# A gated spectral filter and MLP: exchange of partition halves by transfers within SBUF, one unsplit tile, outputs weighed early

## The chip, the cores and the metric

The kernel runs on one core of one Trainium2 chip. A core has five engines with an instruction queue each: PE (TensorE, matrix products into the banks of PSUM), DVE (VectorE), ACT (ScalarE), POOL (GpSimd) and SP (SyncE). SP, ACT and POOL also issue DMA transfers, which 16 DMA engines carry out. The metric is the device time of one execution in microseconds. A shape such as 128x512 is partitions by elements of a partition.

## The reference

The input is one sequence of 2048 tokens of width 512; F is 1792.

```
x = A_x
g = sigmoid((x * gate_w).sum(-1, keepdims=True))
a = irfft2(rfft2(x) * (w_r + 1j * w_i))             # over both axes
b = gelu(x @ w1 + b1) @ w2 + b2                     # tanh form of gelu
return g * a + (1 - g) * b
```

So one branch is a two-dimensional Fourier transform, a product with a filter and the transform back; the other is an MLP; a gate for each token mixes them. All values are fp32.

## The kernel before

**Numbers.** An fp32 operand is split into a high part that the fast product format fp32r holds and a low part, the difference. A product is then three fast matmuls: high by high, high by low, low by high. The high part is made by a copy (`split`, `copy`, L424), the low part by a subtraction (L466). Some products of the transform take plain fp32 operands instead.

**Order.** The kernel writes out all of its work as steps (`add`, `v` for DVE, `a` for ACT, `m` for PE, `dma` and `store` for SP, `acc` for an adding transfer on POOL), each with the tiles that it reads and writes. The string ORDER holds the order in which the numbered steps are emitted, and SLOTS the buffer of each tile. The costs and lags in the calls were for the search that made ORDER; when the kernel runs, each engine takes its own steps strictly in the order given and waits at each for what it reads. The order of one engine against another is set by semaphores alone.

**Tiling.** The 2048 tokens are 16 blocks j of 128. They stand in four chunks c = j mod 4 of 512 tokens: CA is chunks 0 and 1, CB is 2 and 3. F is 14 tiles f of 128, the model width is four quarters q of 128.

**The Fourier branch.** `forward(j)` loads a block (L477, the first two in halves, L502 and L504), adds and subtracts its quarters on DVE (`eo` L575, `w` L578), multiplies by a table `cf` on PE (`pd`, plain fp32), splits that into `zb` (L608, L612) and multiplies by a table for the block (`py`) into Y[j]. The columns of the gate's weights are written into `cf` by a small DVE copy (L529), so that `pd` gives the gate's sums as well; that copy waits for both halves of `cf` (L509). `stage1`, `filt` and `stage4` combine blocks four at a time on DVE. `own_rows` sends partitions 0 and 64 of all Y, which hold special rows, through a small matmul of their own (L636, L652).

`inverse(c, h)` takes two blocks. For each it needs the block with its partition halves 0 to 63 and 64 to 127 exchanged and its two parts (real and imaginary) exchanged: two ACT instructions on 64 partitions with a scale of each partition, which zeroes partitions 0 and 64 (L794), and one on partition 64 alone, whose scale is a cosine (L797), write `sw`; two DVE instructions (L801) form `pq` from y, a factor for each partition, and `sw`. `pz` multiplies `pq` by a table `tg` (plain fp32, table weighed by the gate, L788), ACT and DVE split that into `zb` (L813, L814), `pa` multiplies by the table `ci`, and a few ACT and DVE steps (`od`, `u`, `v`, L838, L842) give a part of the output. For CB it stays in Y; for CA the transfer `w<-bacc` (L409) adds the MLP part to it, and it goes to the output (L848).

**The MLP branch.** `group(s, p)` takes a range of f tiles for s = A (chunks 0, 1) or B (chunks 2, 3). In the first group of A, f = 0 and 1, the product up to F is `plain(c, f)` (`ph`): the three matmuls of the split operands, for c=0 in pieces of 128 and 256 columns as the blocks arrive, for c=1 in one go. All other groups use `seven`, which makes two f tiles for two chunks with seven block products (`nu`, `ux`). `load_w` loads and splits weights (`war` is the raw w1 tile; f=0 comes in two halves, L869, and is cast on DVE, L870). `gelu` runs on ACT. `down(p, c, fs, G)` multiplies by w2: ACT first puts the running sum `s` back into PSUM (`po<-s`, L932), then come the `po` matmuls, and a copy out to `s`. In the last group of B, `last` weighs with 1-g and adds Y in two DVE steps (L962, L971) and stores (L977); the very last tile, chunk 3, q=3, goes in two halves of 256 columns, its second half in two blocks of 128, the last of which is stored from ACT's queue (L975).

**The gate.** A sum, a Sigmoid on ACT (L1137) and a tiny Gelu behind it (L1140), which brings Gelu's table back; then a round through DRAM spreads it to `gb` in all partitions.

**The start.** Nine large matmuls of zeros warm PE up, and five small ones (`none`, FILL) are put between its first steps.

Of the kernel before, what the change touches and what calls it, by code (L numbers as in the profile page):

```python
# [1229 lines left out]
```

## Time and profile before

| | us |
|---|---|
| Median of 3 runs | 358.93 (358.54 to 359.77) |
| The profiled execution | 357.73 |
| Its span, first to last instruction or landing | 355.8 |
| PE's last matmul ends | 351.62 |

| Engine | Busy us | Instructions |
|---|---|---|
| PE matmul | 348.8 | 1770 |
| DVE | 323.1 | 674 |
| ACT | 294.8 | 612 |
| POOL | 38.7 | 52 |

The profile is of one execution. A line number is that of the kernel. A busy PE includes time in which a matmul's end is modelled, so the pace of its starts says more than its busy time. A group row gives the number of instructions, their busy time and mean length in ns, then the idle time of the engine before them and who ended it. Plain fp32 products show two records each. Most matmuls have the line of a helper, 415, and are told apart by their tiles.

### The profile page before, as it was taken

The numbers are of one execution on the slowest core, as the hardware profiler recorded it, in microseconds if no ns is written. First come the engines' busy times: TensorE is split into PE (matmuls) and PEld (weight loads), VectorE is DVE, ScalarE is ACT, GpSimd is POOL, SyncE is SP. The second block draws the span as 40 slices with busy tenths as digits, with TensorE's granted clock in tenths as the row PEclk, the third lists the DMA queues.
The fourth block names the chain that finished last, engine by engine and source line by source line (L and its number), as shares of the span: only waits on it lengthen the run. The fifth ranks groups of instructions, "written<-read, shape, count | busy, mean of one in ns | idle before, by whom it ended". The sixth has DMA issues, their size and how long they took to land.

```text
span 355.8 us, 5738 instructions
## 1 busy us (share of the span) xinstructions
PE 348.8 (98%) x1770; PEld 294.8 (83%) x1770; DVE 323.1 (91%) x674; ACT 294.8 (83%) x612; POOL 38.7 (11%) x52
## 2 busy tenths in 40 slices
PE   7999999999999999999999999999999999999995
PEld 5988888888887888888888888878888888888884
DVE  5999997799999999999999999999989987779856
ACT  4989999999999984996678894589999899999510
POOL 1011101000102200010000400003000000021230
PEclk9999999999999999999999999999999999999999
DMA  7999868937798959997888954479403347345598
GB/s 230 371 270 321 158 191 287 242 125 212 184 277 210 332 115 294 357 272 236 282 274 224 220 110 99 131 261 207 135 7 104 96 134 234 123 106 133 111 201 272
DMA packets 47790, 72.47 MB, mean 204 GB/s; under 512 B 5648, under 2 KB 19472, under 8 KB 47760
## 3 DMA queue, kind: packets, MB, share of 16 engines
q1 hardware_dynamic: 40480, 61.51, 53.0%
q0 software_dynamic: 6848, 10.27, 18.5%
q10 hardware_dynamic: 432, 0.33, 0.3%
q8 instruction: 14, 0.23, 0.2%
q14 instruction: 16, 0.13, 0.1%
HBM read 52.55 MB, written 19.41 MB: 202 GB/s over the span
## 4 chain that ended last, share of the span: by engine, by line
PE 88%; DMA 5%; ACT 3%; DVE 1%; SPq 1%; issue 1%; DVEq 0%; ACTq 0%
PE po L415 39%; PE uxB L415 11%; PE uxA L415 9%; PE nuB L415 8%; PE nuA L415 7%; PE pz L415 4%; PE pa L415 3%; PE pd L415 3%; PE py L415 3%; DMA xbA<-in_xc 2%; DMA wb3l_raw<-in_w 2%; DMA xf<-in_xt 1%; PE ph L415 1%; ACT s L942 1%; DMA xf<-in_x0g 1%
## 5 line engine op out<-in xcount | busy, mean ns | idle before, releaser
L932 ACT ACTIVATE po<-s 128x512 f32<-128x512 f32 (+1 forms) x49 | 28.8, 594 | 8.0 <-DVE t L962 7.4
L424 ACT ACTIVATE s<-po 128x512 f32<-128x512 f32 x40 | 23.8, 597 | 13.1 <-PE po L415 12.8
L794 ACT ACTIVATE sw<-y,al 64x512 f32<-64x512 f32 x32 | 22.5, 718 | 0.5
L755 DVE TENSOR_TENSOR m<-y,wf 128x514 f32<-128x514 f32 x32 | 21.3, 688 | 0.6
L415 PEld LDWEIGHTS pd<-cf,w 128*128 128x128 f32 x128 | 17.7, 190 | 3.7 <-DVE cf L529 2.2
L415 PE MATMUL pd<-cf,w 128*128 128x129 f32 x128 | 19.2, 276 | 1.5 <-DVE cf L529 1.4
L415 PE MATMUL py<-zb,tf 128*128 128x258 f32 x96 | 19.6, 292 | 0.1
L409 POOL DMA_DIRECT2D w<-bacc x8 | 9.6, 1256 | 91.3 <-DVE w L842 81.0
L415 PEld LDWEIGHTS pz<-tg,pq 128*128 128x128 f32 x128 | 17.5, 190 | 1.9 <-issue 0.3
L415 PE MATMUL pz<-tg,pq 128*128 128x128 f32 x128 | 18.6, 275 | 0.0
L415 PEld LDWEIGHTS py<-zb,tf 128*128 128x128 f32 x96 | 15.5, 189 | 2.6 <-ACT zb L608 0.3
L801 DVE SCALAR_TENSOR_TENSOR pq<-y,al,sw 128x256 f32<-128x256 f32 x32 | 15.1, 478 | 2.8 <-ACT sw L794 1.9
L415 PE MATMUL nuB<-xB,wB0h 128*128 128x512 f32 x56 | 17.4, 391 | 0.0
L415 PE MATMUL pa<-zb,ci 128*128 128x256 f32 x96 | 16.2, 290 | 0.0
L415 PEld LDWEIGHTS pa<-zb,ci 128*128 128x128 f32 x96 | 14.0, 189 | 1.7 <-DVE zb L814 0.2
L612 DVE TENSOR_TENSOR zb<-pd,zb 128x256 fp32r<-128x256 f32 x32 | 13.2, 418 | 2.1 <-ACT logit L611 2.0
L415 PE MATMUL nuA<-xA,wA0h 128*128 128x512 f32 x48 | 14.9, 392 | 0.0
L942 ACT ACTIVATE s<-po,b2t 128x512 f32<-128x512 f32 x16 | 10.6, 689 | 5.0 <-PE po L415 5.0
L632 ACT ACTIVATE y<-pys 64x257 f32<-64x257 f32 x32 | 13.0, 416 | 0.8 <-DVE pys L629 0.3
L575 DVE TENSOR_TENSOR eo<-xf 128x256 f32<-128x256 f32 x32 | 12.6, 417 | 0.8 <-DMA xf<-in_x0g 0.4
L608 ACT ACTIVATE zb<-pd 128x256 fp32r<-128x256 f32 x32 | 11.9, 387 | 1.5 <-PE py L415 0.9
L814 DVE TENSOR_TENSOR zb<-pz,zb 128x512 fp32r<-128x512 f32 x16 | 10.9, 686 | 2.0 <-ACT zb L813 2.0
(532 smaller groups left out, 1225.3 us busy)
## 6 DMA issues: line engine op xcount, KB each, us to landing
wf<-in_wf SPq DMA_DIRECT2D x16, 257.0 KB, 3.9
xf<-in_xt SPq DMA_DIRECT2D x14, 256.0 KB, 5.0
tf<-tf SPq DMA_DIRECT2D x16, 192.0 KB, 3.6
wrA<-in_w SPq DMA_DIRECT2D x12, 256.0 KB, 5.5
xbA<-in_xc SPq DMA_DIRECT2D x8, 256.0 KB, 4.2
xbB<-in_xc SPq DMA_DIRECT2D x8, 256.0 KB, 4.8
bacc<-s SPq DMA_DIRECT2D x8, 256.0 KB, 2.8
w<-bacc POOLq DMA_DIRECT2D x8, 256.0 KB, 4.5
```

What stands on the lines that cost most here:

```text
L415: pe.matmul(ps, w, x, start=start, stop=stop, **more)
L424: a(lambda: act.activation(o.ap(), i.ap(), AF.Copy, scale=scale), n, [i], [o])
L575: v(lambda s=s, op=op: vec.tensor_tensor(eo.ap()[:, s], x.ap()[:, 0:2], x.ap()[:, 2:4], op=op), 256, [x], [(eo, s)])
L608: a(lambda c=c: act.activation(segs(xh, c), both(c), AF.Copy), 256, [ps[c]], [(xh, c)])
L612: v(lambda c=c: vec.tensor_tensor(segs(xl, c), both(c), segs(xh, c), op=ALU.subtract), 256, [ps[c], (xh, c)], [(xl, c)])
L632: a(lambda o=o, i=i: act.activation(Y[j].ap()[o:o + HP, 1], pys.ap()[i:i + HP, 1], AF.Copy), 257, [(pys, 1)], [(Y[j], 1 + k)], more=0.1)
L755: v(lambda mk=mk, k=k, y=y, w=w: vec.tensor_tensor(mk.ap(), y.ap(), w.ap()[:, k:k + 1, :ND].to_broadcast([P, 2, ND]), op=ALU.mult), 514, [ ...
L794: a(lambda sw=sw, y=y, o=o, i=i: act.activation(sw.ap()[o:o + HP], y.ap()[i:i + HP, ::-1, :HD], AF.Copy, scale=al.ap()[i:i + HP, 0:1]), 51 ...
L801: v(lambda sw=sw, pq_=pq_, y=y, j=j, k=k, op=op: vec.scalar_tensor_tensor(pq_.ap()[:, k], y.ap()[:, k, :HD], al.ap()[:, 1 + j:2 + j], sw.a ...
L814: v(lambda n=n, ps=ps: vec.tensor_tensor(zl.ap()[:, :, :, n], ps.ap(), zh.ap()[:, :, :, n], op=ALU.subtract), 512, [ps, (zh, n)], [(zl, n)])
L932: a(lambda ps=ps, n=n, o=o: act.activation(ps.ap(), o.ap()[:, n], AF.Copy), size, [o], [ps])
L942: a(lambda o=o, ps=ps, q=q: act.activation(o.ap(), ps.ap(), AF.Identity, bias=b2t.ap()[:, q:q + 1]), 600, [b2t, ps], [o])
```

## The change

- **Exchange by transfers.** In `inverse`, the two L794 and the one L797 of each block give way to two DMA transfers on SP that copy partitions 65 to 127 onto 1 to 63 and back, both parts in their order; POOL zeroes partitions 0 and 64 of `sw` first. `pq` becomes a plain add or subtract that reads `sw` with its parts exchanged.
- **Row 64 turned per chunk.** The rotation of partition 64 that L797 and the factors did is done once for a chunk, at the end of `stage4`: a transfer brings that row of its four blocks to four partitions, one ACT and two DVE instructions turn it, and a transfer writes it back. `pq` waits for that.
- **Tanh gate.** Sigmoid is written as 0.5 tanh(z/2) + 0.5, with a tiny DVE step; the second table call is gone.
- **First f tile unsplit.** `plain(0, 0)` multiplies the raw x by the raw w1 in plain fp32, 16 products of 128 columns, in steps that wait for the raw tiles only. `plain(0, 1)` becomes 12 matmuls of 512 columns. The cast of the f=0 tile goes from DVE to ACT.
- **Last outputs weighed early.** For chunk 3 in the last group, the running sum is weighed and Y subtracted before it goes back into PSUM, and g (the output of `gelu`) is weighed before its split, so that the output is the negative of PSUM: one ACT copy with scale -1 and a store.
- FILL is 3 instead of 5. ORDER and SLOTS are new as a whole, and some costs and lags in the calls differ.

```diff
-    al = np.ones((P, 1 + NJ))
-    al[[0, HP], 0] = 0.0
-    al[HP, 1:] = np.sin(np.pi * np.arange(NJ) / NJ)
+    turn = np.pi * np.arange(NJ).reshape(4, 4) / NJ
+    al = np.stack([np.sin(turn), np.cos(turn)], 2)
...
+    def weighed(name, src, c):
+        x = buf("t2k", [P, 512], F32, f"{name}w", cls="gw")
+        v(lambda: vec.scalar_tensor_tensor(x.ap(), gb.ap()[:, c], 1.0, src.ap(), op0=ALU.subtract, op1=ALU.mult), 512, [gb, src], [x])
+        return split(name, x)
...
-    FILL = 5
+    FILL, WARM, NBARE = 3, 9, 1
...
+        if c == 0:
+            RAW[j // 4] = x
...
     def stage4(j0):
...
+        dma(lambda: sp.dma_start(flat(x.ap()[:4]), rows()), 8, ys, [x], 4.5)
+        a(lambda: act.activation(z.ap()[:4, :, :HD], x.ap()[:4, :, :HD], AF.Copy, scale=al.ap()[:, j0, 1:2]), 512, [x, al], [z], more=0.1)
+        for k, op in enumerate((ALU.subtract, ALU.add)):
+            v(lambda k=k, op=op: vec.scalar_tensor_tensor(
+                x.ap()[:4, k, :HD], x.ap()[:4, k, :HD], al.ap()[:, j0, 0:1], z.ap()[:4, 1 - k, :HD], op0=ALU.mult, op1=op), 256,
+                [z, al], [(x, k)], more=0.055)
+        dma(lambda: sp.dma_start(rows(), flat(x.ap()[:4])), 8, [x, *ys], [row], 4.5)
...
     def inverse(c, h):
...
+            add("pool", 1.0, 0.2, clear, [], [(sw, 2)])
             for k, (o, i) in enumerate(((0, HP), (HP, 0))):
-                a(lambda sw=sw, y=y, o=o, i=i: act.activation(
-                    sw.ap()[o:o + HP], y.ap()[i:i + HP, ::-1, :HD], AF.Copy, scale=al.ap()[i:i + HP, 0:1]), 512,
-                    [y, al], [(sw, k)], more=0.21)
-            a(lambda sw=sw, y=y, j=j: act.activation(
-                sw.ap()[HP:HP + 1], y.ap()[HP:HP + 1, ::-1, :HD], AF.Copy, scale=math.cos(math.pi * j / NJ)), 512,
-                [y], [(sw, 1)], more=0.13)
+                dma(lambda sw=sw, y=y, o=o, i=i: sp.dma_start(sw.ap()[o + 1:o + HP], y.ap()[i + 1:i + HP, :, :HD]), 160, [y], [(sw, k)], 3.4)
             for k, op in enumerate((ALU.subtract, ALU.add)):
-                v(lambda sw=sw, pq_=pq_, y=y, j=j, k=k, op=op: vec.scalar_tensor_tensor(
-                    pq_.ap()[:, k], y.ap()[:, k, :HD], al.ap()[:, 1 + j:2 + j], sw.ap()[:, k], op0=ALU.mult, op1=op), 256,
-                    [y, sw, al], [(pq_, k)], more=0.055)
+                v(lambda sw=sw, pq_=pq_, y=y, k=k, op=op: vec.tensor_tensor(
+                    pq_.ap()[:, k], y.ap()[:, k, :HD], sw.ap()[:, 1 - k], op=op), 256,
+                    [y, TURNED[c], sw], [(pq_, k)])
...
-        if c or f > 1:
+        if c or f >= NBARE:
...
+            def some(j, qs):
                 for q in qs:
+                    mm(ps.ap()[:, j * P:(j + 1) * P], w.ap()[:, q * P:(q + 1) * P], RAW[j].ap()[:, q], j == q == 0, j == qs[0] == 0 and q == qs[-1],
+                       skip_group_check=j + qs[0] > 0)
...
     def down(p, c, fs, G):
...
+                if end and c == CB[-1] and n.start == 0:
+                    v(lambda o=o: vec.scalar_tensor_tensor(o.ap(), gb.ap()[:, c], 1.0, o.ap(), op0=ALU.subtract, op1=ALU.mult), 512, [gb], [o])
...
+                    v(less_y, 512, [(y, q % 2) for y in ys], [o])
...
     def last(c, q, ps, n, tail):
...
+        if c == CB[-1]:
+            if tail and n.start:
+                for k in range(2):
+                    s = slice(k * P, (k + 1) * P)
+                    d = slice(n.start + k * P, n.start + (k + 1) * P)
+                    a(lambda s=s: act.activation(t.ap()[:, s], ps.ap()[:, s], AF.Copy, scale=-1.0), P, [ps], [(t, k)])
+                    if k:
+                        add("act", 0.4, 2.6, lambda s=s, d=d: act.dma_start(dst[:, d], t.ap()[:, s]), [(t, k)], [], P / 680)
+                    else:
+                        store(lambda s=s, d=d: sp.dma_start(dst[:, d], t.ap()[:, s]), P / 2, [(t, k)], [])
+                return
+            copy(t, ps, size, scale=-1.0)
...
-    gate_step = a(lambda: act.activation(gate.ap(), gate.ap(), AF.Sigmoid, scale=0.25), 30, [], [gate])
-    gate_step.table = "sigmoid"
-
-    a(lambda: act.activation(logit.ap()[:, 0, 0, 0:1], gate.ap()[:, 0:1], AF.Gelu_apprx_tanh), 1, [gate], [(logit, 0)]).table = "gelu"
+    a(lambda: act.activation(gate.ap(), gate.ap(), AF.Tanh, scale=0.125), 30, [], [gate]).table = "gelu"
+    tiny(lambda: vec.tensor_scalar(gate.ap(), gate.ap(), 0.5, 0.5, op0=ALU.mult, op1=ALU.add), [], [gate])
```

More of the change, by code (lines that the diff above doesn't have):

```diff
@@ L488, in warm @@
     def warm():
-        for _ in range(9):
+        for _ in range(WARM):
             mm(none.ap(), zero.ap(), bcast(zero.ap(), 4), True, True)
-    add("pe", 3.93, 0.1, warm, [zero], [none])
+    add("pe", 0.09 + 0.427 * WARM, 0.1, warm, [zero], [none])
     for _ in range(FILL):
@@ L635, in forward @@
                 o = j % 4 * 2 + k
-                add("sp", 0.58, 2.8, lambda k=k, o=o: sp.dma_start(own.ap()[o * 8:o * 8 + 8, :ND], yy.ap()[0:P:HP, j % 4::4, k]),
+                add("sp", 0.58, 5.0, lambda k=k, o=o: sp.dma_start(own.ap()[o * 8:o * 8 + 8, :ND], yy.ap()[0:P:HP, j % 4::4, k]),
                     [Y[i] for i in range(j % 4, NJ, 4)], [(own, o)])
@@ L779, in stage4, with flat, rows @@
         radix4(ys, [j0 * q0 for q0 in range(4)], 1, HD, ys, f"d{j0}")
+        x, z = (t2k(f"own{n}{j0}", cls="own", parts=2) for n in "xz")
+        row = TURNED[j0] = one(f"turned{j0}", [1, 1])
+        def flat(t):
+            return t.rearrange("p a b -> p (a b)")
+        def rows():
+            return yy.ap()[HP:HP + 1, j0::4].rearrange("p j a b -> p j (a b)")
+        dma(lambda: sp.dma_start(flat(x.ap()[:4]), rows()), 8, ys, [x], 4.5)
[5 more added lines that the diff above has]
+        dma(lambda: sp.dma_start(rows(), flat(x.ap()[:4])), 8, [x, *ys], [row], 4.5)
     def inverse(c, h):
@@ L858, in halve @@
         minus(h, l, src)
+    BARE = {}
     def load_w(n, f):
         first = n == "a" and f == 0
-        h, l = W[n, f] = [buf("w", [P, D], F32R, f"w{n}{f}{k}", cls=n + k, parts=2 if first and k == "h" else 1) for k in "hl"]
+        h, l = W[n, f] = [buf("w", [P, D], F32R, f"w{n}{f}{k}", cls=n + k) for k in "hl"]
         src = (w1 if n == "a" else w2)[f]
@@ L865, in load_w @@
         t = buf("w", [P, D], F32, f"w{n}r{f}", cls=n + "t", parts=2 if first else 1) if own else None
-        if first:
-            for k in range(2):
-                o = slice(k * HD, (k + 1) * HD)
-                dma(lambda o=o: sp.dma_start(t.ap()[:, o], src[:, o]), 128, [], [(t, k)])
-                v(lambda o=o: vec.tensor_copy(h.ap()[:, o], t.ap()[:, o]), 256, [(t, k)], [(h, k)])
-        elif own:
-            dma(lambda: sp.dma_start(t.ap(), src), 256, [], [t])
+        if own:
+            BARE[f] = t
+            for k in range(2 if first else 1):
+                o, i = (slice(k * HD, (k + 1) * HD), (t, k)) if first else (slice(0, D), t)
+                dma(lambda o=o: sp.dma_start(t.ap()[:, o], src[:, o]), 128 if first else 256, [], [i])
             copy(h, t)
@@ L953, in last @@
     def last(c, q, ps, n, tail):
-        ys = [Y[c + 8 * h + 4 * (q // 2)] for h in range(2)]
         dst = out[c][:, q].rearrange("p a b -> p (a b)")
-        t = buf("w", [P, ps.shape[1]], F32, f"t{c}{q}{n.start}", parts=2, cls="t")
-        some = range(0, ps.shape[1], P) if tail and n.start else (0,)
-        for k, i in enumerate(some):
-            w = ps.shape[1] // len(some)
-            o = [(t, k)] if len(some) > 1 else [t]
-            s = slice(i, i + w)
-            v(lambda s=s, i=i, w=w: vec.scalar_tensor_tensor(
-                t.ap()[:, s], gb.ap()[:, c, n.start + i:n.start + i + w], 1.0, ps.ap()[:, s], op0=ALU.subtract, op1=ALU.mult), w, [gb, ps], o)
-            def minus_(s=s, i=i, w=w):
-                if ps.shape[1] == 4 * P:
-                    y = yy.ap()[:, c + 4 * (q // 2)::8, q % 2, :2 * P]
-                    x = t.ap().rearrange("p (a b) -> p a b", a=2)
-                else:
-                    y, x = ys[n.start // (2 * P)].ap()[:, q % 2, i:i + w], t.ap()[:, s]
-                vec.tensor_tensor(x, y, x, op=ALU.subtract)
-            v(minus_, w, [(y, q % 2) for y in (ys if not tail else ys[n.start // (2 * P):][:1])], o)
-            if k:
-                add("act", 0.4, 2.6, lambda s=s, i=i, w=w: act.dma_start(dst[:, n.start + i:n.start + i + w], t.ap()[:, s]), o, [], w / 680)
-            else:
-                store(lambda s=s, i=i, w=w: sp.dma_start(dst[:, n.start + i:n.start + i + w], t.ap()[:, s]), w / 2, o, [])
@@ new lines, in last, with minus_ @@
+        size = ps.shape[1]
+        t = buf("w", [P, size], F32, f"t{c}{q}{n.start}", parts=2, cls="t")
+        if c == CB[-1]:
[10 more added lines that the diff above has]
+            copy(t, ps, size, scale=-1.0)
+        else:
+            v(lambda: vec.scalar_tensor_tensor(t.ap(), gb.ap()[:, c], 1.0, ps.ap(), op0=ALU.subtract, op1=ALU.mult), size, [gb, ps], [t])
+            def minus_():
+                x = t.ap().rearrange("p (a b) -> p a b", a=2)
+                vec.tensor_tensor(x, yy.ap()[:, c + 4 * (q // 2)::8, q % 2, :2 * P], x, op=ALU.subtract)
+            v(minus_, size, [(Y[c + 8 * h + 4 * (q // 2)], q % 2) for h in range(2)], [t])
@@ L979, in put @@
+        store(lambda: sp.dma_start(dst[:, n], t.ap()), size / 2, [t], [])
     def put(b, e, x):
@@ L1082, in done @@
             gelu(ps, 2 * u + i)
-            G[cs[n], 2 * u + i] = split(f"g{cs[n]}_{2 * u + i}", ps)
+            name = f"g{cs[n]}_{2 * u + i}"
+            G[cs[n], 2 * u + i] = weighed(name, ps, cs[n]) if cs[n] == CB[-1] and 2 * u + i in GROUPS[1][-1] else split(name, ps)
         times(N[0], "11", "11", True)
```

53 lines of the change are left out of this document (29 added, 24 removed), and 200 rows, old and new, of tables (ORDER, SLOTS).

## The prediction

> **What bounds the kernel now.** First the page's busy line and its chain (shares of the span by engine), then the busy times by stretch (columns: stretch, its length, then PE, PEld, DVE, ACT, POOL busy with instruction counts, granted clock, DMA share, GB/s).
>
> ```profile
> PE 348.8 (98%) x1770; PEld 294.8 (83%) x1770; DVE 323.1 (91%) x674; ACT 294.8 (83%) x612; POOL 38.7 (11%) x52
> PE 88%; DMA 5%; ACT 3%; DVE 1%; SPq 1%; issue 1%; DVEq 0%; ACTq 0%
> ...
> 0.00:5.00 5.00, 3.94 (x9) 2.81 (x9) 1.07 (x4) 1.49 (x2) 1.77 (x12) 1.00 0.56 162
> 5.00:10.00 5.00, 3.56 (x29) 3.26 (x28) 4.69 (x19) 3.35 (x13) 0.00 (x0) 1.00 0.93 318
> 130.00:140.00 10.00, 10.00 (x45) 8.26 (x44) 9.83 (x20) 5.69 (x12) 0.84 (x1) 1.00 0.67 177
> 290.00:300.00 10.00, 10.00 (x62) 8.85 (x60) 8.60 (x20) 9.68 (x17) 0.00 (x0) 1.00 0.63 192
> 350.00:356.00 6.00, 1.62 (x14) 1.42 (x12) 2.58 (x8) 0.00 (x0) 0.00 (x0) 0.85 0.66 229
> ```
>
> PE is full in the middle, at clock 1.00, whatever the other engines do; only the two ends are thin. A busy PE could still be slow, so the chain gives its pace (columns: start, length, what).
>
> ```profile
> 15.99 0.48 PE ph L415 x4
> 118.60 19.07 PE po L415 x84
> 265.06 0.89 PE pz L415 x8
> ```
>
> 84 matmuls of 512 columns in 19.07 us are 0.227 each; four of 256 columns in 0.48 are 0.120; a product in plain fp32 of 128 columns has two records, so eight in 0.89 are 0.2225 a product. By the loops of the code PE has 1230 matmuls of 512 columns, 260 of 256 to 258, 128 fp32 products and small ones: 279.2 + 31.2 + 28.5 + 1.4 = 340.3 us. The stream runs from 6.70 to 351.62 (rows below), 344.9 us, so that waits and fillers inside it are worth only about 4.6 us in all, spread thinly. **The bound is PE's work, plus the time before its first useful matmul, plus the time after its last.** DVE and ACT matter only where they stop PE.
>
> The head (timeline: start, length, engine, line, operation):
>
> ```profile
> 0.74 0.39 SPq L504 DMA_DIRECT2D xf<-in_xt  x1
> 1.05 4.21 PE L415 MATMUL none<-zero 128*128 128x512 f32 x9 [1.05 <-DVE zero L483]
> 1.19 0.42 SPq L509 DMA_DIRECT2D cf<-cf  x1
> 2.12 0.43 SPq L509 DMA_DIRECT2D cf<-cf  x1
> 2.60 0.43 SPq L872 DMA_DIRECT2D war<-in_w  x1
> 3.08 0.94 SPq L869 DMA_DIRECT2D war<-in_w  x2
> 6.14 0.43 DVE L575 TENSOR_TENSOR eo<-xf 128x256 f32<-128x256 f32 x1
> 6.48 0.16 DVE L529 COPY cf<-g 128x4 f32<-128x4 f32 x1
> 6.70 0.49 PE L415 MATMUL pd<-cf,w 128*128 128x129 f32 x2 [1.44 <-DVE cf L529]
> 6.94 0.37 PE L415 MATMUL none<-zero 128*128 128x256 f32 x1
> ```
>
> After the warming matmuls PE stands 1.44 us until the copy into cf at 6.48, then starts on pd. Five fillers `none` come between, the first at 6.94. The tail:
>
> ```profile
> 351.34 0.28 PE L415 MATMUL po<-g_13h,wb13lb 128*128 128x256 f32 x1
> 351.66 0.29 DVE L962 SCALAR_TENSOR_TENSOR t<-gb,po 128x128 f32<-128x128 f32 x1
> 351.98 0.29 DVE L971 TENSOR_TENSOR t<-y,t 128x128 f32<-128x128 f32 x1
> 352.50 0.29 DVE L971 TENSOR_TENSOR t<-y,t 128x128 f32<-128x128 f32 x1
> 352.82 0.35 ACTq L975 DMA_DIRECT2D out<-t  x1
> ```
>
> PE ends at 351.62; four DVE instructions, two for each half of the last 256 columns, stand before the last store at 352.82, which ends the span at 355.8.
>
> **The change part by part.**
>
> *First f tile unsplit.* Before: the 28 split matmuls of f=0, c=0 (in `plain`), 20 of 256 columns at 0.120 = 2.4 and 8 of 128 columns, unquoted singly, taken at 0.10 = 0.8, so 3.2 us. After: 4 token blocks x 4 quarters = 16 fp32 products of 128 columns at 0.2225 = 3.56. For f=1, c=0, 24 of 256 (2.88) become 12 of 512 (2.72). PE work is +0.2 us. But the products need only the raw x and raw w1, neither cf nor a split, so they can stand ahead of pd. Counting steps in the new list, PE's order is: warm, first pair, two fillers, second pair, the four of the second block, then pd: 8 products, 1.78 us, before pd. For this the SP order becomes x4, w1, x4, w1, cf, cf; cf moves from the second and fourth place to the fifth and sixth, whose issues began at 2.60 and 3.08 above.
>
> ```profile
> cf<-cf SPq DMA_DIRECT2D x2, 129.0 KB, 3.8
> ```
>
> At 3.8 us from issue to landing the second w1 half, now fourth (2.12), lands at 5.9 and cf, now last (3.08), at 6.9. On DVE the new list puts both eo and one w of the second block before the copy into cf: three at 0.42 where one stood, so the copy, 6.48 before, comes near 7.7 and pd near 7.95, 1.25 later. PE's stream: +1.25 (pd later) - 3.2 (old f=0) + 1.78 (8 products that remain) - 0.16 (f=1) - 0.5 (fillers now in the idle time or gone, some 0.1 each) = **-0.83 us**. Bounds: -1.6 if the copy goes at 7.0, as soon as cf lands; 0 if the DMA engines, 0.93 busy in 5:10, bring cf 0.8 later.
>
> *Last outputs weighed early.* The last two blocks of 128 columns need one ACT copy each from PSUM in place of two DVE instructions.
>
> ```profile
> L611 ACT ACTIVATE logit<-pd 128x2 f32<-128x2 f32 x32 | 5.3, 176 | 0.0
> L608 ACT ACTIVATE zb<-pd 128x256 fp32r<-128x256 f32 x32 | 11.9, 387 | 1.5 <-PE py L415 0.9 <-DVE zb L612 0.4
> ```
>
> Estimated halfway between 2 and 256 columns: 0.28 us, two are 0.56, so the last issue starts near 352.25 in place of 352.82: **-0.55 us**. What it needs earlier, eight 512-wide DVE instructions on the sums (0.69 each, 5.5 us) and four for the weighed g (2.8 us), takes the place of 6.1 us of L962/L971 in the end; it lies on a DVE that has room after 300, and is costed at nothing; without that cover PE would wait for the ACT preload `po<-s` behind it, one 0.69 for each late pair.
>
> *The inverse's exchange.*
>
> ```profile
> L794 ACT ACTIVATE sw<-y,al 64x512 f32<-64x512 f32 x32 | 22.5, 718 | 0.5
> L797 ACT ACTIVATE sw<-y 1x512 f32<-1x512 f32 x16 | 10.0, 628 | 0.4
> L801 DVE SCALAR_TENSOR_TENSOR pq<-y,al,sw 128x256 f32<-128x256 f32 x32 | 15.1, 478 | 2.8 <-ACT sw L794 1.9 <-ACT sw L797 0.8
> L759 DVE TENSOR_TENSOR y<-m,m 128x257 f32<-128x257 f32 x16 | 6.7, 418 | 0.0
> tg<-ti SPq DMA_DIRECT2D x16, 64.0 KB, 1.9
> ```
>
> ACT loses 32.5 us, all between 243 and 325. DVE's 32 pq drop from 478 to some 418 ns (the form of L759): -1.9 us; the row turns add 8 STT (at 478 ns, 3.8 us) and 4 ACT copies. SP gets 32 transfers and 8 row transfers; at 0.42 us an issue (the row of cf) 17 us of its queue, in a stage where it mostly waits. Each exchange then takes a DMA, between 1.9 us (tg, 64 KB) and 3.8 (cf, 129 KB, near its 126 KB); I take 3.4, nearer the equal size. The row of a chunk goes out, is turned and comes back. The nearest row pair for a transfer of single partitions:
>
> ```profile
> 104.00 0.53 SPq L636 DMA_DIRECT2D own<-y  x1
> 108.17 0.19 PEld L415 LDWEIGHTS pown<-own,fx 64*64 64x64 f32 x2 [0.35 <-DMA own<-y]
> ```
>
> 4.2 us; so out 4.2 + ACT 0.6 + DVE 2 x 0.48 + back 4.2 = 10 us from stage4 to pq, where two L794 and one L797 took 2.1. Queued behind a waiting pq on DVE stand the splits and sums of the sevens, which free PSUM for PE. Cover: the same list keeps other DVE work between, counted step by step at 0.42 or 0.69 us each, about 8.6 us between stage4(2) and its first turn, and 4.4 before its pq, against needs of some 5 each. I cost it at nothing, with bounds of -2 (half of the 4.6 us of waits were ACT's) and +4 (next part).
>
> [...] No row here has 63 partitions. [...]
>
> *Tanh gate.* Two table loads go from ACT:
>
> ```profile
> L1137 ACT ACT_TABLE_LOAD x1 | 1.3, 1283 | 0.0
> L1140 ACT ACT_TABLE_LOAD x1 | 1.3, 1283 | 0.0
> ```
>
> 2.6 us on ACT near 100, where PE has its 0.227 pace without it: nothing. The changed lags and costs in the planner's calls change no instruction.
>
> Sum: -0.83 - 0.55 = **-1.4 us**. The profiled execution took 357.73 (span 355.8 and 1.9 around it); the median shown is 358.93, 1.2 above. Set against the median: **357.5 us**.
>
> **The rivals.**
>
> *Middle waits go too (355.6).* ACT was the fullest engine beside PE in 290:300 (9.68); freed of 32.5 us, it answers PE sooner. For it: the wait of pq for sw in L801. Against: PE's windows are full there. At best half of 4.6 us: -1.4 - 2 = 355.5, say 355.6.
>
> *The head gives nothing (358.4).* 5:10 has the DMA engines at 0.93: the same bytes feed PE, and 8 products early only mean that it waits for cf and x later. Then the tail's -0.55 is left: 358.4. For it: pd really waits for cf today; against: PE does have the raw tiles by 5.9.
>
> *The row's round trip is late (slower).* Place: pq on DVE, behind the returned row. It decides once the other DVE work between stage4 and pq is under 10 us for a chunk; if it is 1.2 us short in each of 4 chunks and PE has nothing else in its fixed order, +4.8 - 1.4: 362.3. For it: a fixed order can't step around a late DMA. Against: before, sw began at 243 and pz at 263, 20 us of slack:
>
> ```profile
> L415 PEld LDWEIGHTS pz<-tg,pq x128: 186/192/193, 262.9 to 331.9; 128*128 128x128 f32 x128
> L794 ACT ACTIVATE sw<-y,al x32: 701/722/728, 243.3 to 322.8; 64x512 f32<-64x512 f32 x32
> ```
>
> **How the numbers follow.** Forecast 357.5, own range 356.7 to 358.4 by the head's bounds: 0.50. Middle waits 0.16, head gives nothing 0.21, late row 0.13. The bound of a visible difference is 0.3%, 1.08 us, so faster means under 357.85: four fifths of the forecast's case and all of the middle's, 0.40 + 0.16 = 0.56; slower 0.13; the rest, 0.31, is the same. The range runs from 355.6 to 359.6: it holds the first three cases but for the edge of the second, and leaves out most of the late row.
>
> **What would show it.** Right: fp32 ph matmuls before pd, pd later than 6.7 but the last po matmul near 350.8; the last store issued about 0.6 after it, not 1.2; PE full in 260:330, with ACT well under 9. Wrong: PE idle in 5:10 for longer than 1.4 us; a gap in PE with pq, or the DVE waiting for y or sw by DMA; po waiting for ACT behind the weighed sums in 335:350. I am wrong above all if the waits inside PE's stream, 4.6 us before, become another number.

## The result, and the profile after

The changed kernel takes 363.3 us (median of 4, 362.7 to 364.3); the kernel before took 359.0 (358.5 to 359.8) beside it. The ratio is 1.012, 95% interval 1.0087 to 1.0153: slower by 4.3 us, where 1.4 us less was forecast. The profiled execution is the one of 362.7, span 360.9 (before 357.73 and 355.8).

The page's busy line of the changed kernel, and its busy times by stretch (columns as in the prediction):

```profile
PE 349.3 (97%) x1760; PEld 294.0 (81%) x1760; DVE 324.3 (90%) x681; ACT 266.7 (74%) x572; POOL 54.6 (15%) x84
```

```profile
140.00:165.00 25.00, 23.39 (x102) 18.75 (x101) 21.89 (x43) 18.48 (x39) 2.60 (x3) 1.00 0.92 272
165.00:200.00 35.00, 34.16 (x152) 28.01 (x151) 34.76 (x69) 25.35 (x50) 4.07 (x5) 1.00 0.84 255
285.00:320.00 35.00, 32.85 (x190) 27.76 (x189) 26.87 (x63) 18.00 (x34) 7.24 (x14) 1.00 0.67 195
```

The same stretches of the kernel before:

```profile
140.00:165.00 25.00, 25.00 (x112) 20.71 (x111) 24.57 (x45) 23.00 (x48) 2.58 (x3) 1.00 1.03 327
165.00:200.00 35.00, 35.00 (x156) 29.00 (x155) 34.63 (x66) 25.83 (x51) 2.57 (x3) 1.00 0.81 245
285.00:320.00 35.00, 35.00 (x205) 30.56 (x204) 28.26 (x63) 33.30 (x57) 2.38 (x2) 1.00 0.50 148
```

PE was full in all three and now stands 1.61 + 0.84 + 2.15 = 4.6 us; 10, 4 and 15 matmuls fewer fit in. ACT was relieved as meant, 294.8 to 266.7 us busy. PE's last matmul starts at 355.75 in place of 351.34, 4.4 us later, and from there the span ends 5.1 us later where it took 4.5. So the loss lies in three stretches and at the end, and I take them in turn.

**140 to 165 us.** The timelines of SP, ACT, DVE and PE of the changed kernel, one fence for each:

```profile
127.40 0.42 SPq L880 DMA_DIRECT2D wb13l_raw<-in_w  x1
134.96 1.84 SPq L757 DMA_DIRECT2D wf<-in_wf  x2
...
147.09 1.21 SPq L757 DMA_DIRECT2D wf<-in_wf  x1
```

```profile
155.88 0.21 ACT L758 ACTIVATE wf<-edges 128x4 f32<-128x4 f32 x1 [3.05 <-DMA wf<-in_wf]
155.99 0.58 ACT L423 ACTIVATE s<-po 128x512 f32<-128x512 f32 x1
156.60 0.60 ACT L966 ACTIVATE po<-s 128x512 f32<-128x512 f32 x1
```

```profile
153.43 0.69 DVE L465 TENSOR_TENSOR g_11l<-uxA,g_11h 128x512 fp32r<-128x512 f32 x1 [2.11 <-DMA su<-wAtl]
```

```profile
157.26 0.50 PE L414 MATMUL po<-g_10h,wb10h 128*128 128x512 f32 x1 [1.43 <-ACT po L966]
```

SP stands from 127.8 to 135.0 on a load whose buffer a late VectorE multiply frees, and everything behind it goes out as a burst. The wf load issued at 147.09 is only used at 155.88, 8.8 us later; it stands at the head of ACT's queue, and PE's refill of `po` is two behind it. A store of wAtl that had to read its buffer out holds DVE for 2.11 us in the same burst. None of this is the exchange: its first transfer is issued at 244.8 (below). What differs here from the kernel before is mainly the new ORDER, with its SLOTS.

**165 to 200 us.** One load of the same stretch of the order, wBth, is issued at 184.13 and lands 6.75 us later by the chain of waits, and PE waits 0.8 us for it. Most of the runs below do not show this wait, so it may be chance of this execution.

**285 to 320 us.** The line of the exchange's issues (ns: shortest, median, longest; first and last start), then SP's, DVE's and PE's timelines:

```profile
L823 SPq DMA_DIRECT2D sw<-y x32: 787/808/1097, 244.8 to 308.5; - x32
```

```profile
298.55 0.81 SPq L823 DMA_DIRECT2D sw<-y  x1
299.46 0.48 SPq L810 DMA_DIRECT2D tg<-ti  x1
299.99 0.81 SPq L823 DMA_DIRECT2D sw<-y  x1
```

```profile
303.22 0.29 DVE L811 TENSOR_TENSOR tg<-tg,gb 128x128 f32<-128x128 f32 x1 [0.62 <-DMA tg<-ti]
```

```profile
303.66 0.68 PE L414 MATMUL pz<-tg,pq 128*128 128x128 f32 x4 [0.47 <-DVE tg L811]
```

An exchange's issue takes 0.81 us, and in this stretch they come back to back with loads between. A tg load goes out behind one and is waited for by DVE, and PE waits for DVE. Some tg loads are held by more than the queue: SP stands 12.8 us, in five waits between 240 and 325 us, until PE frees the buffer of the next one. The list of waits of DVE from 140 to 330 us says the same (engine and line, waited for: total, times, longest), of the changed kernel, then of the kernel before:

```profile
DVE tg L811 <- DMA tg<-ti: 3.7, 3, 1.6
DVE pq L825 <- DMA sw<-y: 3.3, 2, 2.2
```

```profile
DVE v L838 <- ACT u L424: 2.1, 2, 1.3
DVE pq L801 <- ACT sw L794: 1.9, 2, 1.4
```

Waits for ACT became waits for DMA.

**The head** went as forecast (PE's timeline): raw products from 4.64, pd at 8.26 where 7.95 was forecast.

```profile
4.64 0.71 PE L414 MATMUL ph<-xf,war 128*128 128x128 f32 x4
6.39 1.58 PE L414 MATMUL ph<-xf,war 128*128 128x128 f32 x12 [0.80 <-DMA war<-in_w]
8.26 1.83 PE L414 MATMUL pd<-cf,w 128*128 128x129 f32 x14 [0.30 <-DVE cf L533]
```

**The tail** went as forecast in its first half (ACT's timeline): two copies of 0.27 us, the last issue 0.52 us after PE's end at 356.03, not 1.2. But the span ends 4.35 us after that issue, before 2.98. SP issues three more stores between 355.27 and the end, of 256, 128 and 64 KB.

```profile
356.07 0.45 ACT L996 ACTIVATE t<-po 128x128 f32<-128x128 f32 x2 [0.33 <-PE po L414]
356.55 0.35 ACTq L998 DMA_DIRECT2D out<-t  x1
```

### The profile page after: what moved, and what is told of

Its sections match the earlier page's. It is cut to its first block, busy times and chain, and to the rows that moved or that the text cites. A ratio compares the mean times of both kernels' runs of the same rounds, so it can differ in the third digit from the quotient of the medians.

```text
span 360.9 us, 5784 instructions
## 1 busy us (share of the span) xinstructions
PE 349.3 (97%) x1760; PEld 294.0 (81%) x1760; DVE 324.3 (90%) x681; ACT 266.7 (74%) x572; POOL 54.6 (15%) x84
## 4 chain that ended last, share of the span: by engine, by line
PE 82%; DMA 8%; SPq 5%; DVE 2%; issue 1%; ACT 1%; POOL 0%; DVEq 0%; POOLq 0%
PE po L414 39%; PE uxA L414 8%; PE uxB L414 8%; PE nuA L414 6%; PE nuB L414 6%; PE pd L414 4%; PE py L414 3%; PE ph L414 3%; SPq L823 2%; DMA wf<-in_wf 2%; PE pz L414 2%; DMA wBth<-su 2%; PE pa L414 2%; DMA g<-in_x0g 1%; DMA sw<-y 1%
## 5 line engine op out<-in xcount | busy, mean ns | idle before, releaser
L819 POOL MEMSET sw<- 1x512 f32 x32 | 16.6, 518 | 27.9 <-PE po L414 15.2
L414 PE MATMUL py<-zb,tf 128*128 128x258 f32 x96 | 20.7, 297 | 0.0
L414 PE MATMUL pa<-zb,ci 128*128 128x256 f32 x96 | 17.3, 289 | 0.6 <-DVE zb L838 0.6
L414 PEld LDWEIGHTS pa<-zb,ci 128*128 128x128 f32 x96 | 15.1, 189 | 2.9 <-DVE zb L838 1.0
L825 DVE TENSOR_TENSOR pq<-y,sw 128x256 f32<-128x256 f32 x32 | 12.8, 417 | 4.2 <-DMA sw<-y 3.3
L837 ACT ACTIVATE zb<-pz 128x512 fp32r<-128x512 f32 x16 | 9.0, 595 | 7.1 <-PE pa L414 4.8
L423 ACT ACTIVATE od<-pa 128x512 f32<-128x512 f32 x8 | 4.8, 598 | 11.9 <-PE pa L414 8.7
L408 POOL DMA_DIRECT2D wA0l<-in_w x6 | 5.4, 956 | 52.2 <-DMA tf<-tf 22.1
```

What stands on the lines that cost most here:

```text
L408: return add("pool", 0.9, 3.8, lambda: nc.gpsimd.dma_start(dst(), src(), accum_op=ALU.add), reads, writes, 2.3 * kb / 340)
L414: pe.matmul(ps, w, x, start=start, stop=stop, **more)
L423: a(lambda: act.activation(o.ap(), i.ap(), AF.Copy, scale=scale), n, [i], [o])
L819: nc.gpsimd.memset(sw.ap()[o:o + 1], 0.0)
L825: v(lambda sw=sw, pq_=pq_, y=y, k=k, op=op: vec.tensor_tensor(pq_.ap()[:, k], y.ap()[:, k, :HD], sw.ap()[:, 1 - k], op=op), 256, [y, TURNE ...
L837: a(lambda n=n, ps=ps: act.activation(zh.ap()[:, :, :, n], ps.ap(), AF.Copy), 512, [ps], [(zh, n)])
```

## The experiments

Theory Q: the exchange's transfers crowd SP's queue and hold tg and sw back. Rival R: the row of `stage4` comes back late and holds pq. Rival M: the loss is made in the middle and at the end by the new order, not by the exchange. Each kernel is the changed one with one edit, unless said otherwise. Ratios are to the kernel before, run beside it on the same chip; the changed kernel's own, 1.012, is 363 us. That one was measured once and not again beside each experiment, so a ratio whose interval overlaps 1.009 to 1.015 is not shown to differ from it. PE's and DVE's idle time is a window's length less the busy time; a PE that runs at a lower granted clock counts as busy (e4, 158 to 160 us: 2.00 of 2.00 us at 0.56):

| Run | Time, us | Ratio, 95% | PE idle 140:165 | PE idle 250:285 | PE idle 285:320 | DVE idle 140:165 |
|---|---|---|---|---|---|---|
| before | 359.0 | 1 | 0.00 | 0.00 | 0.00 | 0.43 |
| changed | 363.3 | 1.012 (1.009 to 1.015) | 1.61 | 0.00 | 2.15 | 3.11 |
| e1 copies on ACT | 379.0 | 1.058 (1.055 to 1.061) | 2.26 | 5.68 | 5.48 | 4.09 |
| e2 half on ACT's queue | 362.8 | 1.012 (1.010 to 1.014) | 2.17 | 0.00 | 0.96 | 4.07 |
| e3 64 partitions | 364.9 | 1.016 (1.013 to 1.020) | 1.68 | 0.69 | 2.19 | 2.89 |
| e4 no row turn | 361.9 | 1.010 (1.006 to 1.014) | 2.14 | 0.00 | 0.55 | 3.81 |
| e5 wf6's edges later | 362.6 | 1.012 (1.010 to 1.014) | 0.55 | 0.98 | 2.27 | 2.78 |
| e6 tg ahead | 367.7 | 1.027 (1.026 to 1.029) | 2.21 | 3.99 | 2.27 | 4.19 |
| e7 stores ahead | 362.3 | 1.014 (1.012 to 1.015) | 0.99 | 0.58 | 2.93 | 2.89 |
| e9 e5 and e6 | 367.2 | 1.025 (1.024 to 1.026) | 0.66 | 3.57 | 1.76 | 2.88 |
| e12 e7 and e2 | 361.4 | 1.010 (1.008 to 1.012) | 1.30 | 0.56 | 0.64 | 3.17 |

The profile is of one execution; the runs of one kernel differ by 1 to 5 us (e4: 359.3 to 364.1), so a stretch shows a mechanism, and only the ratio a price.

### The exchange

The old copies in the new order:

```diff
-                dma(lambda ...: sp.dma_start(sw.ap()[o + 1:o + HP], y.ap()[i + 1:i + HP, :, :HD]), ...)
+                    act.activation(sw.ap()[o:o + HP], y.ap()[i:i + HP, ::-1, :HD], AF.Copy, scale=al.ap()[i:i + HP, 0:1])
+                    if k:
+                        act.activation(sw.ap()[HP:HP + 1], y.ap()[HP:HP + 1, ::-1, :HD], AF.Copy, scale=math.cos(math.pi * j / NJ))
```

> The changed kernel with the old exchange put back at the same places of the order: two ScalarE copies and the one-row copy per chunk, the row turned inside pq, no transfers and no clears. Theory Q (the transfers crowd SP's queue: 32 issues of 0.81 us and 8 of 0.65 hold tg and sw back): the waits of PE on tg, zb and pq between 285 and 320 us (1.3 + 0.6 + 0.2) go, about 2 to 3.5 us, so 360.0 to 361.3. Theory R (the turned row comes back late and holds pq): the same, since the row goes too. Theory M (the loss is made in the middle of the kernel and at its end by the new order, 150 to 160, 184 to 191 and the last stores): 362.7 to 363.3, no change.

Measured 379.0, 16 us worse, outside every theory. The list of waits of this kernel shows why:

```profile
PE pa L415 <- ACT od L424: 6.8, 2, 4.4
```

The copies stand in ACT's order where transfers could stand, ahead of the copies of `od`, and PE waits 6.8 us for those. The idle time is not all: in the table's three stretches the granted clock was 0.93, 0.95 and 0.85, which is about 8.8 us of PE's work (0.07 of 25 us, 0.05 of 35 and 0.15 of 35). An order fits one set of durations; this run prices the mismatch and says nothing on Q, R or M. It does show the 140:165 stall without any exchange transfer.

Half of the transfers on another queue:

```diff
-sp.dma_start(sw.ap()[o + 1:o + HP], ...)
+(sp, act)[k].dma_start(sw.ap()[o + 1:o + HP], ...)
```

> Of each chunk's two half transfers the second is issued from ScalarE's queue instead of SP's; all else as in the changed kernel. Theory Q: 16 issues of 0.81 us leave SP, 13 us of the 26; tg lands in time again and 1 to 2.5 us are won, so 360.8 to 362.3; ScalarE, which is busy 267 us, carries the issues without a new wait of PE. Theory R and theory M: no change, 363.3 plus or minus 0.5; where ScalarE's copies before PE come later by the issues, slower.

Alone it gave no change in the median, though PE idles 0.96 us at 285 to 320 where it idled 2.15: the execution lost more at 140 to 165 (2.17 us idle for 1.61, and a granted clock of 0.93 for 1.00; more at the end of this document). An issue costs as much on ACT's queue:

```profile
L823 ACTq DMA_DIRECT2D sw<-y x16: 797/797/1432, 248.7 to 316.8; - x16
```

The odd shape; the zeroing of partitions 0 and 64 is left out with it, so that those two rows come out wrong:

```diff
-sp.dma_start(sw.ap()[o + 1:o + HP], y.ap()[i + 1:i + HP, :, :HD])
+sp.dma_start(sw.ap()[o:o + HP], y.ap()[i:i + HP, :, :HD])
```

> The half transfers take all 64 partitions of a half instead of 63, and the clears go: rows 0 and 64 of sw then hold the other half's rows 0 and 64 instead of zeros, so these two rows enter pq with a term that the reference does not have. It prices the odd shape. If the 63 partitions cost the 0.81 us of issue and the long landing, an issue falls towards the 0.55 us of the wf loads (128 partitions of two pieces), 8 us of SP's time go, and 1 to 2 us of the time by theory Q: 361.3 to 362.3. If the issue stays at 0.8 us, the cost lies in a transfer from SBUF to SBUF and not in the count of partitions, and the time stays at 363 plus or minus 0.5.

```profile
L822 SPq DMA_DIRECT2D sw<-y x32: 590/607/1971, 244.1 to 308.3; - x32
```

The 63 partitions cost 0.2 us of each issue, 6.4 us of SP's queue in all, and yet the time did not fall, and PE's idle time at 285 to 320 stayed at 2.19. So the length of the issues alone is not what holds the stretch; the form of Q that counts issue time is not borne out.

The row:

```diff
-        dma(lambda: sp.dma_start(flat(x.ap()[:4]), rows()), 8, ys, [x], 4.5)
+        dma(lambda: None, 8, ys, [x], 4.5)
...
-        dma(lambda: sp.dma_start(rows(), flat(x.ap()[:4])), 8, [x, *ys], [row], 4.5)
+        dma(lambda: None, 8, [x, *ys], [row], 4.5)
```

> The turn of row 64 is left out (two transfers, one ScalarE and two VectorE instructions per chunk): row 64 enters the inverse unturned. Theory R: pq no longer waits behind the returned row, most of the loss between 285 and 320 us goes, 359.8 to 361. Theory Q: 8 issues of 0.65 us leave SP, worth 0 to 0.7 us: 362.5 to 363.3. Theory M: 363.3.

361.9 lies between the theories; the ratio's interval overlaps the changed kernel's, so the row's price is 0 to 2 us and not settled. Its one profile shows PE idle 0.55 us at 285 to 320, not 2.15. The changed kernel's lists of waits show no pq waiting for the returned row, but SP stands before it can issue that return (L802): 4.7 us in two waits between 240 and 325 us. So the row may cost through SP's queue; that it carries most of the loss, as R wanted, is not shown.

The tg loads ahead of the transfers, one of 13 moves:

```diff
-... 1409 1396 2038 1620 2039 1061 1774 1383 1963 1333 1337 1629 2094 1301 1617 ...
+... 1409 1396 2038 1620 2039 1617 1061 1774 1383 1963 1333 1337 1629 2094 1301 ...
```

> Thirteen of the sixteen tg loads of the changed kernel go 2 to 42 steps earlier in SP's order, ahead of the half transfers that stood between the release of their buffer and them; the same transfers in all. Theory Q in its narrow form (the loss of 285 to 320 us is tg standing behind sw on SP's queue): tg's waits on VectorE (3.7 us) go and PE's idle time of 285 to 320 us falls from 3.9 to 1 to 1.8 us: 360.8 to 362. Rival: SP then blocks on the release of tg's buffer, sw is late in place of tg and pq waits: 362.5 to 364.5.

Some 5 us slower by the ratios. SP's timeline of the changed kernel, then SP's, DVE's and PE's of this one, and DVE's list of waits:

```profile
263.81 0.81 SPq L823 DMA_DIRECT2D sw<-y  x1
267.01 0.32 SPq L810 DMA_DIRECT2D tg<-ti  x1
```

```profile
267.44 0.33 SPq L817 DMA_DIRECT2D tg<-ti  x1
267.81 0.81 SPq L830 DMA_DIRECT2D sw<-y  x1
```

```profile
270.60 0.43 DVE L832 TENSOR_TENSOR pq<-y,sw 128x256 f32<-128x256 f32 x1 [4.71 <-DMA sw<-y]
```

```profile
271.68 0.71 PE L421 MATMUL pz<-tg,pq 128*128 128x128 f32 x4 [3.57 <-DVE g_2l L472]
```

```profile
DVE pq L832 <- DMA sw<-y: 7.6, 4, 4.7
```

SP stands until 267.4 on a tg buffer that PE has not freed, as it did in the changed kernel, but now a sw transfer stands behind that load instead of ahead of it. So sw goes out at 267.81 and not at 263.81, pq waits 4.71 us for it, and PE 3.57 for a DVE instruction behind pq. All waits of pq for sw are 7.6 us, in the changed kernel 3.3. The rival held, harder than I expected. What SP's queue costs here is its order, a wait at its head, rather than its issue time.

All transfers on GpSimd's queue (with the five stores of e7):

```diff
-sp.dma_start(sw.ap()[o + 1:o + HP], ...)
+nc.gpsimd.dma_start(sw.ap()[o + 1:o + HP], ...)
```

> The same five stores ahead, and all 32 half transfers from GpSimd's queue, so that none of their issues is on SP's. Theory Q: tg no longer waits behind sw and the second stretch costs 1.5 us or less: 357.8 to 359.5. Rival: GpSimd's queue takes longer for each (its accumulating loads cost it 1.2 us each) and its order holds sw back behind the clears and the accumulating loads; pq waits on sw: 361 to 366.

367.4, ratio 1.027 (1.023 to 1.030): the rival. POOL's list of waits shows a head that waits, now on that queue:

```profile
POOL sw L830 <- PE pa L421: 12.5, 1, 12.5
```

DVE still waits 3.6 us for a tg load, though no issue of sw is left on SP's queue: SP stands 23.8 us there, in eight waits, until PE frees the buffers of tg. So sw ahead of tg on the queue is not the whole of what makes tg late.

### The middle

```diff
-... 1696 1180 878 1171 1486 1166 1463 1031 1492 966 1127 ...
+... 1696 878 1171 1486 1166 1463 1031 1492 966 1180 1127 ...
```

> One 0.2 us ScalarE instruction of the changed kernel, the four-column write into wf6, goes eight steps later in the order, behind the refill of po that PE waits for at 157 us; nothing else. Theory M (part of the loss is this one landing, 8.8 us after its issue, at the head of ScalarE's queue): the wait of PE at 154 to 157 us falls from 2.2 us (2.0 to 4.3 in the runs so far) to under 0.7, 360.0 to 361.8. Rival: VectorE's m waits for the same landing and holds g_12l and the rest, the wait only moves: 363 plus or minus 0.7.

The wait of PE fell to 0.55 us, and the time stayed. PE now loses 0.98 at 250 to 285. DVE's list of waits from 140 to 200 us shows what had not gone:

```profile
DVE g_11l L472 <- ACT wB L1082: 1.5, 1, 1.5
DVE xbB L1026 <- DMA xbB<-in_xc: 1.1, 1, 1.1
```

VectorE still lost 2.6 us. The time is the rival's: the wait moved. Next, the stores in front of the load on which SP stands:

```diff
-... 1001 1083 997 1173 ...
+... 1001 1083 997 801 911 954 955 952 1173 ...
```

> Five stores of the changed kernel whose data are ready go in SP's order ahead of the wf2 load on which SP stands from 127.8 to 135.0 us with the DMA engines empty at 132 to 136; nothing else. Theory L (the first loss is made by these late transfers twice over: wf6 lands after 8.8 us and holds ScalarE, and the late store of wAtl holds VectorE for 2.1 us, which has no slack before 285 us): PE's idle time of 140 to 165 us goes from 2.2 (to 4.3) to under 0.5 and does not come back at 250 to 285: 359.8 to 361.3. Theory M' (VectorE and the later stages give it back, as when only the write into wf6 was moved): 362.3 to 363.3.

```profile
136.49 0.32 SPq L1092 DMA_DIRECT2D su<-wAsl  x1
```

My claim that all five were ready was wrong: SP now stands until 136.49 on the store of wAsl, the fourth, and DVE waits 2.8 us for the late wf. The time is the changed kernel's. Theory M' held, though the edit did not clear what it meant to. Two at a time:

> Both moves together: the write into wf6 eight steps later and the tg loads ahead. If the two losses are separate the gains add: 358 to 360.5. If the second stretch gives back what the first wins, 361 to 363.

367.2, above both ranges: e6's loss with nothing gained. And the stores with half of the transfers on ACT's queue:

> The same five stores ahead, and the second half transfer of each chunk from ScalarE's queue. If the two losses (140 to 165 us and 285 to 320 us) are separate and both come from SP's queue, PE's idle time of 285 to 320 us is 2.5 us or less beside a first stretch near 0: 358.3 to 360.3. If SP's queue is not what holds the second stretch: as with the stores alone.

361.4, the best of the new order, and above the range I gave for success. It is 0.9 us under e7, measured on the same chip, with intervals that just touch; against the changed kernel the intervals overlap. Its profiled execution shows PE idle 0.64 us at 285 to 320, as e2's showed 0.96. This points to SP's queue for about 1 us of the second stretch, but e2's unchanged time speaks against it, so it is not shown; the rest of the loss stays.

### Who sets the pace

That won waits came back asked for a test of the engines themselves: more work for PE or DVE at 205 us, in both kernels.

```diff
+    more = g.steps[1706]    # 1556 for VectorE; 1698 and 1548 in the kernel before
+    more.emit = lambda once=more.emit: [once() for _ in range(3)]    # 5 for VectorE
```

> The changed kernel with one group of six matmuls at 205 us (nuB from wB0h, 1.36 us) issued three times instead of once: 2.7 us more of TensorE's work in the same bank, which the last of them rewrites whole. If TensorE itself sets the time at 205 us, the kernel takes 2.6 to 2.9 us more: 365.6 to 366.4 where the changed kernel gives 363.0 (1.012 to 1.014 of before). If VectorE and the transfers set it (theory V: what TensorE gains ahead of 285 us it waits for afterwards), the 3.9 us that it idles at 285 to 320 us take most of it in: 363.0 to 364.3.

> The changed kernel with one VectorE subtraction at 207 us (g_9l, 0.6 us of its pace) issued five times instead of once, each writing the same: 2.4 us more of VectorE's work. Theory V: VectorE is busy 99% from 170 to 260 us and its lag reaches the transfers, so the kernel takes 1.6 to 2.6 us more: 364.6 to 365.8. If VectorE has slack: under 0.7 us, 363.0 to 363.7.

> The kernel before with the same six matmuls at its own 205 us issued three times: 2.7 us more of TensorE's work. TensorE idles 1.5 us in all from 200 us on there, so 360.6 to 361.0 where before gives 358.0. If VectorE sets the pace in the kernel before as well: under 359.3.

> The kernel before with the same VectorE subtraction at its own 206 us issued five times: 2.4 us more of VectorE's work. VectorE idles 6.9 us from 280 to 330 us there while TensorE waits 0.9 us, so most of it is taken in: 358.0 to 359.2. If VectorE sets the pace in the kernel before as in the changed one: 359.6 to 360.5.

| Added | Changed kernel | Kernel before |
|---|---|---|
| PE, 2.7 us | 364.5, ratio 1.017 (1.014 to 1.020) | 360.7, 1.008 (1.006 to 1.010) |
| VectorE, 2.4 us | 365.5, 1.021 (1.019 to 1.024) | 360.6, 1.008 (1.005 to 1.010) |

In the kernel before both pass on, whole within the noise: 0.8% of 358.4 is 2.8 us, by the intervals 1.8 to 3.6. d4 missed my expectation, by which VectorE's idle time later would take it in. PE feels it at once (the windows 200 to 250 of the kernel before and of d4, then of the changed kernel and of d2):

```profile
200.00:250.00 50.00, 49.87 (x221) 40.89 (x220) 48.66 (x96) 38.80 (x70) 6.93 (x8) 1.00 0.67 161
```

```profile
200.00:250.00 50.00, 48.57 (x212) 39.18 (x211) 48.58 (x94) 36.29 (x65) 6.93 (x8) 1.00 0.65 152
```

```profile
200.00:250.00 50.00, 50.00 (x222) 41.44 (x221) 49.34 (x95) 36.71 (x67) 4.36 (x7) 1.00 0.70 181
```

```profile
200.00:250.00 50.00, 47.35 (x203) 38.70 (x202) 49.13 (x91) 33.39 (x62) 3.81 (x6) 0.97 0.62 173
```

In the changed kernel VectorE's 2.4 us cost some 3, as theory V had it, and in d2's profile part of that is the clock, at 0.97 in a window in which PE idled 2.65 us. PE's 2.7 cost some 1.8 (1.017 less 1.012), between the two expectations, and the intervals of that difference are wide. So at 205 us the kernel before shows no slack on either engine, and the changed kernel none on VectorE. A microsecond that VectorE loses there is about a microsecond of the kernel. This would also explain why e5 won nothing, as it took PE's wait away and left VectorE's; at 155 us it was not tested.

### The end and the head

```diff
-                acc(lambda w=w: w.ap(), lambda k=k: bacc[c].ap()...
+                (acc if c else skip)(lambda w=w: w.ap(), lambda k=k: bacc[c].ap()...
```

> The four accumulating loads of chunk 0 are left out, so out[0] lacks bacc0; all else is as in the changed kernel. In the changed kernel the end comes 5.1 us after PE's last matmul starts (before: 4.4), with the DMA engines full from 344 us on. If the backlog of the DMA engines sets the end, 1 MB less shortens this stretch to 4 us or under: 361.5 to 362.5. If the last store's own chain sets it (copy, issue, landing), it stays at 5 us: 362.8 to 363.8.

362.3, ratio 1.013 (1.011 to 1.014): the loads took no time that shows, and from the start of PE's last matmul, 356.62, to the end of the span, 361.5, there were 4.9 us instead of 5.1. The DMA engines had run nearly empty there (a share of 0.03 at 350 to 352 us) and were full again only from 354 on. So the long end needs no backlog from before 352 us; the last stores alone may make it. The last product but one stored earlier, on e12's kernel (its slot in SLOTS changed too):

```diff
-... 2080 2106 ... 2112 2101 2102 1843 2075 2081 2113 2108 2082 1839 2083 2114 2109 2110 2084 ...
+... 2080 2081 2082 2106 ... 2112 2083 2101 2102 2084 1843 2075 2113 2108 1839 2114 2109 2110 ...
```

> The kernel with the five stores ahead and half of the transfers on ScalarE's queue, with one more change: the last product but one (q = 0 of the last chunk, 256 KB) is finished and stored about 1.5 us earlier, ahead of an accumulated output's store, in place of 1.1 us before the last store. If that store's place holds the end: from PE's last matmul to the end 4.3 to 4.6 us instead of 5.1, so 360.6 to 361.0 where the kernel without it gave 361.4. If the chain of the last store itself or the backlog of all transfers holds it: 361.2 to 361.8.

361.9, ratio 1.009 (1.007 to 1.012); 5.6 us from the last matmul's start, 355.69, to the end, 361.3. The place of that store is not it. What holds the end stays open; the DMA engines, full there, are the candidate. In the changed kernel their share after the last issue at 356.55 is 1.03 up to 358 us and 0.28 up to 360; in the kernel before, after the issue at 352.82, it is 0.91 up to 354 and 0.02 behind it. The changed kernel's window just ahead of that:

```profile
350.00:356.00 6.00, 6.00 (x38) 5.25 (x36) 1.88 (x3) 1.78 (x4) 0.00 (x0) 1.00 1.10 275
```

The head alone on the kernel before, twice:

```diff
-11 16 9 15 0 2 1 60 ... 57 495 27 56 39 ... 58 492 59 490 491 493 20 18 19 110 12 ...
+11 490 9 492 16 15 12 13 64 36 495 110 0 2 1 60 ... 57 27 56 498 499 500 39 ... 58 59 491 493 20 18 ...
```

> The kernel before with one part of the change: the first f tile of the first 512 tokens as unsplit products of the raw tiles, put ahead of the first pd, with its loads earlier on SP; exchange, gate and last outputs as before. The step of the prediction on the head gave 0.83 us, the trace of the changed kernel shows 1.8 us less idle time of PE up to 40 us for 0.4 us more work: 356.8 to 357.6 where before gives 358.2. Rival (the shorter head only brings PE to a later wait sooner, since VectorE has no slack from 100 to 250 us): no change, 358 to 358.5.

361.3, ratio 1.010 (1.008 to 1.011). I had moved the second weight tile's load late and left its ACT copy in place; PE waited 2.6 us behind it, and the granted clock was 0.96 up to 40 us. In that time PE did 1.9 us less work than in the kernel before by its busy time, and the clock took about 1.6 more (0.04 of 40 us); the whole kernel lost 3.4, so the head's loss reached the end. Mended, with that copy and its products later:

> The head alone on the kernel before, as in the earlier run, with what held it there mended: the second weight tile's copy, which stood at the head of ScalarE's queue behind a load moved late, and the products that need it go later in the order. If the head's gain passes to the end on the old order: PE's idle time up to 40 us falls from 8.1 to 6 to 7 us and the time is 356.6 to 357.6 where before gives 358.2. Rival: VectorE, which was not given less to do, holds the next stage and the gain is lost by 100 us: 357.9 to 358.5.

358.0 against 358.3, ratio 0.9983 (0.9968 to 0.9998): in time the rival's range, though the ratio is just clear of 1. The windows of the mended kernel, and of the kernel before:

```profile
0.00:10.00 10.00, 8.86 (x48) 7.83 (x49) 5.85 (x23) 4.06 (x13) 1.76 (x12) 1.00 0.81 248
10.00:40.00 30.00, 29.22 (x180) 25.38 (x180) 29.64 (x78) 28.05 (x79) 4.02 (x5) 1.00 0.93 287
```

```profile
0.00:10.00 10.00, 7.51 (x37) 6.07 (x37) 5.76 (x22) 4.84 (x15) 1.77 (x12) 1.00 0.75 240
10.00:40.00 30.00, 29.86 (x187) 26.48 (x187) 29.84 (x80) 27.77 (x77) 4.24 (x5) 1.00 0.95 289
```

1.35 us more of PE are used up to 10 us, and 0.64 given back by 40, where VectorE is busy 29.6 of 30 us and PE waits 0.7 us for it. It is the one version ahead of the kernel before, by 0.2%, less than the 0.3% that the prediction took as visible.

## Why the prediction was wrong

- **The sum had no term for new waits of PE, and this step failed.** It took "DVE and ACT matter only where they stop PE" and the 4.6 us of waits as all that could change, and added up -0.83 and -0.55. The changed kernel's PE stands 4.6 us more in three stretches that were full. VectorE beside the full PE had no slack (d4, at 205 us: 2.4 us more cost about 2.8), so that late transfers could stop PE through it. The prediction's own last sentence named that as the way to be wrong. The next two points are the places where the term is missing.
- **The exchange, costed "at nothing",** failed: PE stands 2.15 us at 285 to 320, behind late tg, zb and pq (1.3, 0.6 and 0.2 us). The issue, taken at 0.42 from cf's row, is 0.81, so 32 take 26 us of SP; but shorter issues won nothing (e3). That SP's queue has room "in a stage where it mostly waits" was the error: what stands behind a wait of SP is late (in e6 a sw goes out at 267.81, behind a tg load that waited until 267.4, in place of 263.81). The stretch's 2.15 us lies inside the stated bounds of -2 and +4, but the step took 0 from them. How much of the time the exchange costs was not isolated; e12 points to about 1 us for its place on SP's queue.
- **The new order was not priced at all.** Each step of the diff had a cost, and ORDER, which moves every load, had none. The stall at 140 to 165 us, 1.61 us of PE's time, lies 80 us before the first exchange and in every run of that order, e1 and e4 too, though PE idles less there in e5, e7, e9 and e12. What it costs the time was not isolated, as e5 and e7 did not clear VectorE's part. No run puts the exchange into the old order, so the split of the loss between order and exchange stays open.
- **The rival of the late row** named the right sign and stage, but the wait that it named, pq for the returned row, is in no list. The row's return held SP's queue, and e4 leaves its price at 0 to 2 us. Its sum, 362.3, came near 363.3 without that wait, which is luck.
- **The head** was right in mechanism: pd at 8.26 for 7.95. On the old order the gain is 0.3 to 0.6 us of the 0.83 (e16), with an interval of 0.1 to 1.1. On the new order it can't be told from the rest.
- **The tail's -0.55** was right up to the last issue, which came 0.68 us sooner after PE's end, and wrong after it: 4.35 us from there to the end, not 2.98. The step took the landing as fixed. The tail became 0.7 us longer; why stays open.
- **The 63 partitions.** The landing was taken at 3.4 us from rows of 64 and 129 KB, none of which has 63 partitions. The pq in e6 that waited for a sw began 2.8 us after the start of its issue; from GpSimd's queue the median to landing in e15 is 4.7 us. What the runs also show is the issue, 0.81 against 0.61 us with 64, a cost that the estimate did not have.
- **The tanh gate, pq (417 ns for 418) and the row's turn (468 for 478)** were sized right, and the weighed sums did cost PE nothing at 320 to 345 us (25.00 of 25 us busy).

## What to carry to other kernels

Where an order is written out, price the order: list each queue's transfers with what they wait for, since a wait at a queue's head delays what stands behind it, as on SP's queue here (e6: a sw 4.0 us later, a wait of pq of 4.71). Before calling an engine free beside a full one, ask what a microsecond of it would cost; a short test with an instruction issued several times answers that (d4: 2.4 us of VectorE cost about 2.8). And before moving an engine's work to transfers, ask who will wait for them: here ACT got 28.1 us less to do, and VectorE waited 3.7 us for tg and 3.3 for sw.
